# Issuing each group of TensorE products in one piece in a decode attention and bilinear MLP kernel

## The chip, the cores and the metric

The kernel runs on one core of one Trainium2 chip. Times are device microseconds (us) of that core. Profiles are single executions, and each is marked fast or slow. On one core a run is called slow when it is over 1.5% above the fastest run of the same kernel. The granted clock of TensorE in the records is 1.0 or 0.5, and its mean over an execution is given beside the span.

## The reference, cut to what matters

Two tokens (B=2, one query each) go through attention over a cached context and through a bilinear MLP, forward and backward. All tensors are bf16.

```python
# D = 576, Hq = 32, Hkv = 16, Sk = 4096, Dh = 128, F = 4608
xn = layernorm(x)
q  = (xn @ wq).reshape(B, 1, Hq, Dh)
p  = softmax(q @ k_cache^T * Dh**-0.5)      # two query heads share a cache head
y  = x + (p @ v_cache) @ wo + ((xn @ w_gate) * (xn @ w_up)) @ w_down
# returned: y and, by jax.vjp with grad_out, the gradients of
# x, k_cache, v_cache, wq, wo, w_gate, w_up, w_down
```

In all 92.48 MB are read and 92.48 MB written. The two caches and their two gradients are almost three quarters of that, 67.1 MB each way; the weights and their gradients are nearly all the rest. Per step (4 cache heads of one batch entry, 16 steps) TensorE does four things that matter here:

- **scores**: a full-array product (128 rows, 128 columns) of a cache tile that VectorE has transposed, in halves of 16 products, 2048 in all;
- **contractions**: the weighted sum over the cache (128 rows, 32 columns), 64 products each, 32 of them;
- **outer products**: the gradient of the cache (32 rows, 128 columns), in units of 8, each copied out of PSUM by ScalarE or VectorE and then written;
- pieces of the **weights'** work, of several shapes.

Rows and columns are those of the array that a product uses. Where they differ from one product to the next, I call it a change of shape. From the last product before it to the first one after it, start to start, the traces show a longer gap than between products of one shape: 147 to 149 ns at full clock and 241 ns at half (medians, kernel before). I call that gap a drain. That is a name for the time alone: what TensorE does in it isn't shown.

## The kernel before

The code is Python that builds an instruction list. A scheduler puts each engine's instructions in order, so the loops below don't say what lies next to what on TensorE. In particular, the scores of a slot, the outer units queued with `more(2)` and the contraction all feed one queue.

```python
def head_scores(n, t, x, s_ps, half):
    X = xtile([P, NCH, 64], "X")                       # 3 buffers
    t32(...)                                           # VectorE transposes half a cache tile
    for e in range(2):
        be = 2 * half + e
        for c8 in range(8):                            # 16 products, 128 rows x 128 columns
            nc.tensor.matmul(s_ps[:], lhsT=view(W[t][:], ...), rhs=view(X[:], ...), start=..., stop=...)

def contract(rowsT, heads):
    o_ps = ps_m([P, Dh])                               # "m": 2 buffers in PSUM
    for c4 in range(4):
        for c8 in range(8):
            for x, head in enumerate(heads):           # 64 products, 128 rows x 32 columns
                cg = 2 * x + c8 % 2
                nc.tensor.matmul(o_ps[32 * cg:32 * cg + 32, :], lhsT=view(rowsT[:], ...),
                                 rhs=head[:, 8 * c4 + c8, :], start=..., stop=...)
    ...                                                # copied out; the cache tiles come free

def unit(x, ch, A):                                    # one outer unit
    def f():
        ...
        o = ps_o()                                     # 2 buffers of 128 x 1024
        for c in range(4):
            for aa in range(2):                        # 8 products, 32 rows x 128 columns
                a = 2 * A + aa
                nc.tensor.matmul(o[:, aa, c * Dh:(c + 1) * Dh], lhsT=rows[32 * a:32 * a + 32, 4 * ch + c, :],
                                 rhs=bd[32 * a:32 * a + 32, x * Dh:(x + 1) * Dh], start=True, stop=True)
        evac(st[...], o[:], 1024)                      # ScalarE or VectorE
        if ch == 1 and A == 1:
            nc.gpsimd.dma_start(oview[b, :, :, l0 + x]..., st[:]...)
    return f

def slot(src, t, b, l, s_ps, per, mid=None):
    n = head_load(src, b, l)                           # 1 MB of cache, 12 buffers
    head_scores(n, t, l % 2, s_ps, 0)
    more(2)                                            # two outer units
    if mid:
        mid()                                          # softmax or contraction of earlier heads
    head_scores(n, t, l % 2, s_ps, 1)
    more(2)
    other(per)                                         # a piece of the weights' work
    return n
```

(Arguments are cut where "..." stands.)

## Time and profile before

| | before |
|---|---|
| runs at first | 550.19, 550.38, 558.83 us |
| profiled execution | 561.93 us (span 560.2), slow, mean clock 0.766 |
| TensorE products / changes of shape in its order | 8921 / 684 |
| pieces that the 32 contractions are issued in | 76 |
| pieces that the 128 score halves are issued in | 254 |

The three counts are taken from the built instruction list in TensorE's order. Strictly, 684 counts the stretches of one shape; the changes between them are one fewer, 683. The same holds for every such count from a built list below. The lines of the profile are in the prediction below.

### The profile page before, as it was taken

The page shows a single profiled execution, that of the slowest core. Times are in us where ns is not written, and L with a number is a line of the kernel's source. Part 1 is how long each engine was busy: PE and PEld are TensorE (multiplying, and loading weights), DVE is VectorE, ACT ScalarE, POOL GpSimd, SP SyncE. Part 2 cuts the span into 40 slices and gives each one's busy share as a digit, 9 for nine tenths or more (in the row PEclk, how much of TensorE's full clock was granted, in tenths as well). Part 3 has the DMA queues.
Part 4 walks back from the last instruction along what each step waited for, and adds up shares of the span by engine and source line. Part 5 has one row for each costly group of instructions (what it writes and reads, how often), then busy time and mean ns, then how long its engine had stood idle before and what let it go on. Part 6 is the DMA issues. An engine that isn't in the chain of part 4 may idle for free.

```text
span 560.2 us, 20059 instructions
## 1 busy us (share of the span) xinstructions
PE 475.7 (85%) x8921; PEld 362.5 (65%) x8921; DVE 362.0 (65%) x624; ACT 330.6 (59%) x454; POOL 204.6 (37%) x372
## 2 busy tenths in 40 slices
PE   0588988998989999888989899998888999879873
PEld 0476766776776677666767667776776757767630
DVE  8685655757657646458575675668676646577564
ACT  1135695857566465567565665667555566566553
POOL 5125252432622521624235243344243243351322
PEclk9988798877787555688787975589888566798955
DMA  8993999999699998699997999979979889764546
GB/s 254 411 385 135 355 412 368 397 381 405 227 403 393 384 366 324 213 388 379 353 391 253 417 415 375 393 279 411 392 294 390 356 291 403 283 239 171 219 152 245
DMA packets 52911, 186.26 MB, mean 333 GB/s; under 512 B 4140, under 2 KB 19128, under 8 KB 44632
## 3 DMA queue, kind: packets, MB, share of 16 engines
q1 hardware_dynamic: 28392, 92.49, 44.3%
q0 software_dynamic: 24432, 92.48, 43.0%
q8 instruction: 70, 1.15, 0.8%
q14 instruction: 17, 0.14, 0.1%
HBM read 92.48 MB, written 92.48 MB: 330 GB/s over the span
## 4 chain that ended last, share of the span: by engine, by line
PE 31%; ACT 9%; issue 5%; DVE 4%; POOL 2%; POOLq 0%; DVEq 0%; ACTq 0%
PE ps_sc L503 11%; ACT so L93 8%; PE ps_o L549 6%; PE ps_m L518 4%; PE ps_m L527 1%; POOL prm L533 1%; PE ps_m L440 1%; PE ps_o L681 1%; DVE so L90 1%; PE ps_o L651 1%; DVE sto L90 1%; PE ps_m L272 1%; PE ps_o L364 1%; PE ps_m L618 1%; DVE X L102 1%
## 5 line engine op out<-in xcount | busy, mean ns | idle before, releaser
L93 ACT CAST so<-ps_o 128x1024 bf16<-128x1024 f32 x232 | 225.1, 1019 | 125.5 <-PE ps_o L549 114.0
L503 PE MATMUL ps_sc<-X,W 128*128 128x128 bf16 x2048 | 197.2, 249 | 5.3 <-DVE X L102 4.5
L102 DVE STREAM_TRANSPOSE X<-kv 128x1024 f32<-128x1024 f32 x128 | 157.6, 1233 | 44.1 <-PE ps_sc L503 42.7
L503 PEld LDWEIGHTS <-W 128*128 128x128 bf16 x2048 | 153.1, 112 | 27.7 <-issue 17.5
L553 POOL DMA_DIRECT2D out_dram<-so x64 | 50.0, 781 | 138.5 <-ACT so L93 74.6
L549 PE MATMUL ps_o<-bd,dsm 32*128 32x128 bf16 x1024 | 50.9, 245 | 10.3 <-ACT so L93 5.8
L518 PE MATMUL ps_m<-kv,rowT 128*32 128x128 bf16 x2048 | 59.3, 272 | 0.0
L549 PE MATMUL ps_o<-bd,prm 32*128 32x128 bf16 x1024 | 46.3, 250 | 14.3 <-POOL prm L533 7.0
L518 PEld LDWEIGHTS <-rowT 128*32 128x32 bf16 x2048 | 43.0, 121 | 10.0 <-issue 5.8
L549 PEld LDWEIGHTS <-dsm 32*128 32x128 bf16 x1024 | 30.4, 104 | 24.8 <-issue 18.4
L549 PEld LDWEIGHTS <-prm 32*128 32x128 bf16 x1024 | 27.8, 105 | 26.8 <-issue 13.5
L533 POOL TENSOR_TENSOR prm<-pr,maskc 128x1024 bf16<-128x1024 bf16 x16 | 30.2, 1888 | 36.5 <-DVE pr L580 36.5
L93 ACT CAST stw<-ps_o 128x1024 bf16<-128x1024 f32 x28 | 27.8, 1028 | 13.8 <-PE ps_o L364 12.6
L474 POOL COPY dM<-qd 128x128 bf16<-128x128 bf16 x32 | 9.3, 289 | 73.1 <-PE ps_m L480 46.2
L90 DVE CAST so<-ps_o 128x1024 bf16<-128x1024 f32 x24 | 29.1, 1211 | 8.7 <-PE ps_o L549 8.2
L467 POOL COPY W<-rep 32x16 bf16<-32x16 bf16 x128 | 24.7, 193 | 26.1 <-PE ps_sc L503 18.9
L533 POOL TENSOR_TENSOR dsm<-ds,maskc 128x1024 bf16<-128x1024 bf16 x16 | 30.2, 1889 | 4.6 <-DVE ds L600 4.0
L93 ACT CAST std<-ps_o 128x576 bf16<-128x576 f32 x36 | 22.8, 646 | 12.6 <-PE ps_o L397 12.4
L102 DVE STREAM_TRANSPOSE Xw<-wgu 128x1152 f32<-128x1152 f32 x18 | 24.5, 1360 | 4.1 <-PE ps_sc L503 4.0
L93 ACT CAST sto<-ps_o 128x576 bf16<-128x576 f32 x25 | 15.6, 642 | 14.1 <-PE ps_o L681 13.9
L719 DVE TENSOR_SCALAR oT<-ps_m 128x4 bf16<-128x4 f32 x16 | 2.7, 171 | 29.6 <-PE ps_m L527 29.6
L371 POOL DMA_DIRECT2D out_dram<-stw x18 | 13.5, 752 | 19.0 <-ACT stw L93 10.6
(178 smaller groups left out, 591.8 us busy)
## 6 DMA issues: line engine op xcount, KB each, us to landing
out_dram<-so POOLq DMA_DIRECT2D x64, 1024.0 KB, 9.5
kv<-in_A_k_cache_dram SPq DMA_DIRECT2D x32, 1024.0 KB, 11.8
kv<-in_A_v_cache_dram SPq DMA_DIRECT2D x32, 1024.0 KB, 10.1
out_dram<-stw POOLq DMA_DIRECT2D x18, 512.0 KB, 9.3
wd<-in_B_w_down_dram SPq DMA_DIRECT2D x9, 576.0 KB, 12.7
out_dram<-std POOLq DMA_DIRECT2D x9, 576.0 KB, 7.9
wo<-in_A_wo_dram SPq DMA_DIRECT2D x4, 1152.0 KB, 13.4
wgu<-in_B_w_gate_dram SPq DMA_DIRECT2D x9, 512.0 KB, 14.0
```

What stands on the lines that cost most here:

```text
L90: nc.vector.tensor_copy(out=out, in_=in_)
L93: nc.scalar.copy(out, in_)
L102: nc.vector.transpose(out, in_)
L272: nc.tensor.matmul(dp[32 * gq:32 * gq + 32, 0:P], lhsT=view(Wm[:], 0, P, 8 * pos(q, s), [[1, 32]]), rhs=view(X[:], 0, P, koff(s) * 256 + ( ...
L371: nc.gpsimd.dma_start(out[0:512, f0:f0 + FS].rearrange("(c p) n -> p c n", p=P), st[:])
L467: nc.gpsimd.tensor_copy(view(W[t][:], 32 * a, 32, 28 + 32 * a, [[2 * WW, 4], [WW + 2, 2], [1, 2]]), view(st["rep"][:], 32 * a, 32, t * 4 * ...
L474: nc.gpsimd.tensor_copy(view(dM[:], 0, P, t * 2 * P, [[P + 2, 2], [4, 32], [1, 2]]), view(st["qd"][:], 0, P, (2 if t == 0 else 1) * GH * 2 ...
L503: nc.tensor.matmul(s_ps[:], lhsT=view(W[t][:], 0, P, (be * 2 + x) * WW + 28 - 4 * c8, [[1, P]]), rhs=view(X[:], 0, P, c8 * 64 + e, [[8 * 6 ...
L518: nc.tensor.matmul(o_ps[32 * cg:32 * cg + 32, :], lhsT=view(rowsT[:], 0, P, c4 * 32 + 4 * c8, [[1, 32]]), rhs=head[:, 8 * c4 + c8, :], sta ...
L533: nc.gpsimd.tensor_tensor(m[:], view(rows[:], 0, P, 0, [[0, 8], [1, P]]), view(maskc[:], 0, P, 0, [[1, 8], [0, P]]), ALU.mult)
L549: nc.tensor.matmul(o[:, aa, c * Dh:(c + 1) * Dh], lhsT=rows[32 * a:32 * a + 32, 4 * ch + c, :], rhs=bd[32 * a:32 * a + 32, x * Dh:(x + 1) ...
L553: nc.gpsimd.dma_start(oview[b, :, :, l0 + x].rearrange("a m n -> m a n"), st[:].rearrange("p a c d -> p a (c d)"))
```

## The change

Every group of products is wrapped in a `Block`. Its first product is issued as before. The others are issued after it and at top priority, so the scheduler has no reason to put another ready product between them. The aim is fewer changes of shape. The core of the diff:

```diff
+    class Block:
+        def __init__(self):
+            self.first, self.stack = None, ExitStack()
+        def __enter__(self):
+            return self
+        def __call__(self, *args, **kwargs):
+            ins = nc.tensor.matmul(*args, **kwargs)
+            if self.first is None:
+                self.first = ins
+                self.stack.enter_context(tc.issue_after(ins.ins))
+                self.stack.enter_context(tc.high_priority())
+        def __exit__(self, *exc):
+            self.stack.close()
 ...
-        for e in range(2):
-            be = 2 * half + e
-            for c8 in range(8):
-                nc.tensor.matmul(s_ps[:], ...)
+        with Block() as mm:
+            for e in range(2):
+                be = 2 * half + e
+                for c8 in range(8):
+                    mm(s_ps[:], ...)
 ...      (the same for contractions, outer units and every group of the weights' work)
```

All these products now have the line of the helper in the profile, so they are told apart by their tiles: `ps_sc<-X,W` is a score, `ps_m<-kv,rowT` a contraction, `ps_o<-bd,prm` or `ps_o<-bd,dsm` an outer product.

## The prediction

> **What bounds the kernel now.** The times come first: 550.19, 550.38 and 558.83 us. The profiled run took 561.93 us (span 560.2) and is marked slow, so the 550.38 that I predict against belongs to a quicker execution than the one I read, by about 11 us. Then the page, for the balance of the engines:
>
> ```profile
> PE 475.7 (85%) x8921; PEld 362.5 (65%) x8921; DVE 362.0 (65%) x624; ACT 330.6 (59%) x454; POOL 204.6 (37%) x372
> PEclk9988798877787555688787975589888566798955
> q1 hardware_dynamic: 28392, 92.49, 44.3%
> q0 software_dynamic: 24432, 92.48, 43.0%
> ```
>
> Two resources are near full: TensorE (85% busy, with the granted clock falling to 0.5 for long stretches) and the 16 DMA engines. The packets of all queues take 44.3 + 43.0 + 0.8 + 0.1 = 88.2% of the span, 494 us. In the trace a packet of 8192 bytes takes 309 ns in almost every stretch, so these 494 us are occupancy and not queueing. The span can hardly fall below 494 us plus the start and the tail, whatever TensorE does.
>
> Third, the waits, to see which of the two leads, first those of all engines and then those of the load queue:
>
> ```profile
> ACT so L93 <- PE ps_o L549: 114.0, 94, 4.9
> DVE X L102 <- PE ps_sc L503: 42.7, 36, 4.7
> PEld L549 <- issue: 32.0, 99, 0.8
> PEld L503 <- issue: 17.5, 72, 0.7
> PE ps_o L549 <- ACT so L93: 11.7, 27, 0.8
> PE ps_o L549 <- POOL prm L533: 7.0, 6, 1.4
> ...
> SPq L491 <- PE ps_m L518: 208.9, 19, 20.4
> ```
>
> ScalarE and VectorE wait for TensorE; TensorE waits for others little (11.7 and 7.0 us are its largest waits after the start); and the loads of the cache wait 208.9 us for buffers that the contraction (L518) frees. No compute engine waits for a load worth naming. So TensorE leads, and the DMA engines follow at a distance of a few per cent. The busy table by stretch (columns: stretch; busy time and count of PE, PEld, DVE, ACT, POOL; granted clock; DMA share; GB/s) gives that distance:
>
> ```profile
> 20.00:480.00 460.00, 412.94 (x7695) 317.72 (x7699) 295.08 (x492) 285.22 (x395) 171.37 (x315) 0.76 0.93 354
> 192.00:233.00 41.00, 38.17 (x649) 28.36 (x649) 21.52 (x39) 24.21 (x32) 16.03 (x26) 0.58 0.86 318
> 500.00:560.00 60.00, 42.59 (x813) 28.11 (x813) 36.63 (x65) 32.03 (x41) 18.43 (x25) 0.69 0.54 199
> ```
>
> The DMA share is 0.93 over the long middle, 0.86 where the clock is 0.58, and 0.54 in the tail, which only writes. Fourth, the timeline of the weight loads in a slow-clock stretch:
>
> ```profile
> 200.63 0.34 PEld L364 LDWEIGHTS <-xnr 32*128 32x128 bf16 x8 [0.20 <-issue]
> 201.17 0.56 PEld L503 LDWEIGHTS <-W 128*128 128x128 bf16 x6 [0.20 <-issue]
> 201.92 0.34 PEld L364 LDWEIGHTS <-xnr 32*128 32x128 bf16 x8 [0.20 <-issue]
> 202.46 0.56 PEld L503 LDWEIGHTS <-W 128*128 128x128 bf16 x6 [0.20 <-issue]
> ```
>
> Each time the products change from the full array (128*128) to 32 rows (32*128) and back, the weight loads pause 0.20 us and wait for nothing that the profile shows. A score half of 16 products is cut here into pieces of 6, and every cut pays twice.
>
> [...] From the last product of one shape to the first of the next, start to start, the median is 147 ns at full clock and 241 ns at half, against 58 and 104 ns between neighbouring full-array products, 26 and 43 between outer products, 14 and 25 in a contraction. [...] the clock records are 1.0 or 0.5 in multiples of 3.413 us, 76 or so windows at half and 80 at full. I sorted the windows by what followed. Half-clock windows followed by full clock (24) held 2.75 shape changes and 20 full-array products on average; those followed by half again (52) held 4.85 changes and 11. So cut-up stretches seem to hold the clock down; that is a correlation, not yet a cause. [...] the wait of ScalarE for TensorE (114.0 us) against 11.7 us the other way shows that evacuation is not what binds today.
>
> **The change part by part.** No product, copy or transfer is added or removed. Within a block, each product after the first must be issued after it and at top priority, so nothing slips between. I compared the two issue orders, classing each product by the rows and columns it uses. Runs of one kind of product go from 887 to 658; runs of ps_sc products become whole halves of 16 (before: 254 runs for 128 halves), and the contractions whole pieces of 64 (before: 76 runs for 32). Changes of shape go from 684 to 490: 194 fewer. The order of loads on their queue is unchanged.
>
> Drains saved: 365 of the old changes fell at full clock and 318 at half. Excess over ordinary spacing: 147 - (58+26)/2 = 105 ns at full, 241 - (104+43)/2 = 167 ns at half; weighted 0.53 x 105 + 0.47 x 167 = 134 ns. 194 x 0.134 = 26 us of TensorE's queue.
>
> Clock: with 28% fewer changes I expect the mean clock of a comparable run to go from 0.77 to about 0.81. Of 460 us in the middle, 5% is 23 us of TensorE time. As only a correlation carries it, I count 10 us. Together 36 us of relief on TensorE.
>
> What of it reaches the end: in the middle the DMA share can rise from 0.93 to about 1.02 (the table shows 1.02 for 14 to 28 us), which caps the gain at 460 x (1 - 0.93/1.02) = 41 us in the profiled run, and at some 30 us in a quick one, which has already used 11 of them. Of 36 us under a cap of 30, with the queues never perfectly fed, I take half: 15 us. The tail: its changes also fall (about 2 us), but in the new order outer products lag the contractions, by 1 to 13 units at each contraction, and 2.75 more of them stand behind the last one. At 1.02 us of ScalarE copy each that is 3 us. Net -15 - 2 + 3 = -14 us: about 536 us.
>
> **The rivals.** First, DMA takes over at once. The 494 us of packets speak for it; against it stands that no engine waits for a load today. It would leave 5 to 8 us of gain: 543 to 546 us, loads landing late as the new wait. Second, evacuation takes over. The new order issues outer units mostly in pairs (146 bursts of two against 108, and single units 45 against 136); a pair needs both ps_o buffers, and its copies take 2 x 1.02 = 2.04 us, while 16 scores, 16 outer products and two changes take 16 x 0.058 + 16 x 0.026 + 2 x 0.147 = 1.64 us at full clock. TensorE would then wait 0.4 us a pair, 146 x 0.4 = 58 us at the very worst, most of what was gained; but at half clock the same pair takes 16 x 0.104 + 16 x 0.043 + 0.48 = 2.83 us, so copies bind only where the clock is up, and contractions lie between. That gives 540 to 555 us. Third, the small products of the softmax chain (maximum, bias, sum) now wait for the end of a block: 4 per step, 16 steps, half a block of about 0.9 us each, 29 us of latency. Most of it is hidden behind the outer products queued meanwhile; waits of the mask (POOL prm, 36.5 us on DVE pr) would grow. Fourth, on the good side, the clock stays up nearly everywhere and the middle runs at the DMA limit: 517 to 522 us.
>
> **Range and chances.** Point 536 us. The low end, 517, is the whole 30 us of the middle and a little of the tail; the high end, 553, is the second rival with an unlucky clock. Faster by over 2% means under 539.4 us, only 3 us above my point, so 0.57; within 2%, where the first two rivals lie, 0.38; slower than 561.4 would need waits larger than all that is saved: 0.05.
>
> **What would show it.** Right: about 490 changes of shape; "issue" idle before the weight loads of outer and score products clearly under 32.0 and 17.5 us; a mean clock above 0.77 and no stretch of 40 us at 0.6; DMA share of the middle at 0.97 or more; a tail no shorter than now. Wrong: if the clock stays at 0.77 with fewer changes, the correlation was not a cause; if TensorE's wait for ScalarE's copies grows from 11.7 us to 40 or more, pairs took back the gain; if transposes start to wait for cache loads, DMA took over earlier than I allow; and if "issue" idle doesn't fall, the order on the chip is not the one I counted.

## The result, and the profile after

The changed kernel ran in 521.49, 524.13, 525.22 and 526.14 us: median **524.67 us**. The ratio to the kernel before is **0.949**, with a 95% interval of 0.940 to 0.958. A ratio here is the mean time of one kernel's fast runs over that of the other's fast runs of the same rounds, so it is not quite the ratio of the medians. The point predicted was 536 us and the range 517 to 553.

The profile of before is a slow execution. For a comparison I use the profile of a variant, the first experiment below, which has the block helper without the priority. Its TensorE order is the order of before, product for product, its time is the same (ratio 1.004) and its profiled execution is fast. I call it the old order. Here are the page of the old order and that of the changed kernel, each with the busy lines, the clock in 40 slices and the two large DMA queues (packets, MB, share of the 16 engines' span):

```profile
span 549.5 us, 20059 instructions
...
PE 460.2 (84%) x8921; PEld 351.7 (64%) x8921; DVE 360.7 (66%) x624; ACT 329.8 (60%) x454; POOL 204.7 (37%) x372
...
PEclk9998697978796655758798787599789997899555
...
q1 hardware_dynamic: 28392, 92.49, 45.5%
q0 software_dynamic: 24432, 92.48, 43.3%
```

```profile
span 519.7 us, 20063 instructions
...
PE 420.8 (81%) x8921; PEld 336.3 (65%) x8921; DVE 359.8 (69%) x624; ACT 327.5 (63%) x454; POOL 205.4 (40%) x372
...
PEclk9989999679959778796588995889898988799755
...
q1 hardware_dynamic: 28392, 92.49, 47.5%
q0 software_dynamic: 24432, 92.48, 45.0%
```

The other engines do the same work in the same time; TensorE is busy 39 us less. The deep dip of the clock in the middle of the old order (slices of 5 and 6) is gone. The busy table by stretch shows it, for the old order and then for the changed kernel (columns as in the prediction: stretch; PE, PEld, DVE, ACT, POOL; clock; DMA share; GB/s):

```profile
192.00:233.00 41.00, 38.18 (x635) 28.12 (x633) 21.65 (x39) 24.44 (x33) 14.97 (x24) 0.58 0.88 321
20.00:450.00 430.00, 382.42 (x7475) 295.88 (x7477) 281.99 (x474) 271.57 (x378) 164.85 (x301) 0.81 0.95 359
```

```profile
192.00:233.00 41.00, 35.32 (x790) 28.64 (x789) 28.64 (x50) 29.60 (x39) 16.91 (x30) 0.87 0.97 376
20.00:450.00 430.00, 365.96 (x7846) 298.48 (x7847) 294.44 (x499) 280.56 (x394) 173.53 (x316) 0.85 0.98 379
```

From 192 to 233 us the old order does 635 products at clock 0.58; before, in its slow execution, did 649 at the same 0.58, so this dip belongs to the order. The changed kernel does 790 there at 0.87, with less busy time. Over any 40 us of the middle the clock records of the old order fall to 0.50 at the lowest (from 183 us on), those of the changed kernel to 0.67. The DMA share of the middle rises from 0.95 to 0.98.

The waits (engine, line, what it waited for: us in total, times, longest), the old order first:

```profile
ACT so L114 <- PE ps_o L96: 111.8, 92, 5.0
PEld L96 <- issue: 87.2, 263, 2.3
...
POOL prm L566 <- DVE pr L614: 33.9, 16, 7.3
...
PE ps_o L96 <- ACT so L114: 17.1, 41, 1.1
```

```profile
PEld L93 <- issue: 91.7, 196, 3.8
...
ACT so L112 <- PE ps_o L93: 60.0, 71, 3.4
...
PE ps_o L93 <- ACT so L112: 20.5, 45, 1.2
...
POOL prm L564 <- DVE pr L612: 15.1, 12, 5.9
...
DVE Xd L121 <- DMA wd<-in_B_w_down_dram: 9.9, 2, 6.6
...
DVE X L121 <- DMA kv<-in_A_k_cache_dram: 5.4, 3, 2.8
```

ScalarE now waits for TensorE 60.0 us where it waited 111.8, and TensorE for ScalarE hardly more than before, 20.5 against 17.1. The mask on GpSimd waits less for the softmax, not more. VectorE now waits for loads before it transposes: 9.9 us for the weight tile `wd`, 2.2 in the old order, and 5.4 us for cache tiles, none there. The pauses called "issue" are fewer (196 against 263), but their sum didn't fall.

The timeline of weight loads in a stretch of the changed kernel at half clock (start, us, engine, line, operation, tile, count, idle time before) shows blocks kept whole:

```profile
208.46 1.75 PEld L93 LDWEIGHTS <-W 128*128 128x128 bf16 x16
210.40 0.37 PEld L93 LDWEIGHTS <-dsm 32*128 32x128 bf16 x16 [0.20 <-issue]
```

Where before had pieces of 6 scores and 8 outer products with a pause at each joint, there are 16 and 16 with one pause.

**TensorE's queue, added up.** I cut the time from the first product's start to the last one's into the gaps from start to start. A gap between products of one shape counts as stream, a gap at a change of shape as drain, one after an fp32 product apart; whatever a gap has over 65 ns (stream) or 155 ns (drain) at full clock, 110 or 250 at half, counts as stall. These caps are my choice, set just above the medians of the traces. In us:

```
                 first-last   stream (at full, at half)   drain (changes: full, half)   fp32   stall
before (slow)       541.8     294.7  (146.6, 148.2)       129.7  (376, 307)             20.1    97.3
old order           531.2     282.6  (166.1, 116.5)       123.1  (450, 233)             19.7   105.8
changed             501.3     283.7  (189.1,  94.6)        86.2  (371, 118)             20.4   111.0
```

From the old order to the changed kernel: drains -37, stream +1, stalls +5, in all -30 us. The medians of a gap at a change of shape stay what they were, 147 to 149 ns at full and 241 ns at half clock. The drains fell by more than the 28% of the changes because fewer of the remaining ones fall at half clock: 118 of 489, against 233 of 683.

### The profile page after: what moved, and what is told of

The parts are those of the page before. It is cut to its first block, busy times and chain, and to the rows that moved or that the text cites.

```text
span 519.7 us, 20063 instructions
## 1 busy us (share of the span) xinstructions
PE 420.8 (81%) x8921; PEld 336.3 (65%) x8921; DVE 359.8 (69%) x624; ACT 327.5 (63%) x454; POOL 205.4 (40%) x372
## 3 DMA queue, kind: packets, MB, share of 16 engines
q0 software_dynamic: 24432, 92.48, 45.0%
HBM read 92.48 MB, written 92.48 MB: 356 GB/s over the span
## 4 chain that ended last, share of the span: by engine, by line
PE 46%; DVE 16%; ACT 15%; DMA 9%; issue 9%; SPq 3%; POOL 1%; POOLq 0%; DVEq 0%; ACTq 0%
PE ps_sc L93 17%; ACT so L112 13%; PE ps_o L93 12%; PE ps_m L93 11%; DVE X L121 5%; DMA wd<-in_B_w_down_dram 4%; DMA out_dram<-so 3%; DVE so L109 2%; SPq L317 2%; PE ps_m L558 2%; DVE x_f L168 1%; DMA wgu<-in_B_w_gate_dram 1%; DVE Xd L121 1%; ACT stw L112 1%; PE ps_m L509 1%
## 5 line engine op out<-in xcount | busy, mean ns | idle before, releaser
L93 PE MATMUL ps_sc<-X,W 128*128 128x128 bf16 x2048 | 159.0, 236 | 13.4 <-issue 6.7
L93 PEld LDWEIGHTS <-W 128*128 128x128 bf16 x2048 | 141.4, 106 | 21.1 <-issue 14.5
L93 PE MATMUL ps_m<-kv,rowT 128*32 128x128 bf16 x2048 | 44.0, 250 | 3.8 <-issue 3.2
L93 PEld LDWEIGHTS <-rowT 128*32 128x32 bf16 x2048 | 36.8, 112 | 6.5 <-issue 4.3
L564 POOL TENSOR_TENSOR prm<-pr,maskc 128x1024 bf16<-128x1024 bf16 x16 | 30.3, 1891 | 15.2 <-DVE pr L612 15.1
L93 PEld LDWEIGHTS <-Wdy 128*128 128x128 bf16 x306 | 22.3, 111 | 4.6 <-POOL dM L503 3.1
L396 POOL DMA_DIRECT2D out_dram<-stw x18 | 13.7, 759 | 29.0 <-ACT stw L112 13.9
L555 ACT COPY o_sb<-ps_m 128x128 f32<-128x128 f32 x32 | 8.6, 269 | 25.1 <-PE ps_m L93 24.8
## 6 DMA issues: line engine op xcount, KB each, us to landing
out_dram<-so POOLq DMA_DIRECT2D x64, 1024.0 KB, 10.6
```

The lines of the kernel that those rows point to most:

```text
L93: ins = nc.tensor.matmul(*args, **kwargs)
L396: nc.gpsimd.dma_start(out[0:512, f0:f0 + FS].rearrange("(c p) n -> p c n", p=P), st[:])
L555: nc.scalar.copy(o_sb[:], o_ps[:])
L564: nc.gpsimd.tensor_tensor(m[:], view(rows[:], 0, P, 0, [[0, 8], [1, P]]), view(maskc[:], 0, P, 0, [[1, 8], [0, P]]), ALU.mult)
```

## The experiments

Twelve kernels ran, in three groups on the same chip each with runs of before beside them. The expectations name theories by letter. In short: theory A puts the gain down to the number of changes of shape alone; C to how the outer units lie between the contractions; D to the cuts inside contractions. B was a rival of A in the first group, and both expected a gain from scores alone. Groups differ by chip: e1 to e8 ran on one chip, e9 to e12 on another. A table of what came out; the changes and the pieces are counted in the built instruction list:

| label | blocks whole | changes | contraction pieces | median us | ratio to before [95%] | profiled span, clock |
|---|---|---|---|---|---|---|
| before | none | 684 | 76 | 551 to 555 | 1 | 560.2, 0.766 (slow) |
| after | all | 490 | 32 | 524.67 | 0.949 [0.940, 0.958] | 519.7, 0.840 |
| e1 | none, edge only | 684 | 76 | 555.27 | 1.004 [0.994, 1.015] | 549.5, 0.809 |
| e2 | scores | 615 | 109 | 558.46 | 1.006 [0.996, 1.016] | 555.3, 0.806 |
| e3 | contractions | 652 | 32 | 534.29 | 0.962 [0.953, 0.972] | 533.6, 0.824 |
| e4 | all but outer | 495 | 32 | 520.92 | 0.941 [0.933, 0.950] | 520.6, 0.853 |
| e9 | all but contractions | 593 | 111 | 552.76 | 0.997 [0.988, 1.005] | 550.9, 0.787 |
| e10 | scores and contractions | 548 | 32 | 534.76 | 0.967 [0.959, 0.975] | 531.3, 0.819 |

**e1: the ordering edge without the priority.**

```diff
                 self.stack.enter_context(tc.issue_after(ins.ins))
-                self.stack.enter_context(tc.high_priority())
```

> The blocks keep their ordering edge (each product after the first must follow the first) but lose the top priority. By the instruction order it is the kernel before, product for product: 684 changes of array shape. If the contiguity does the work: the same time as before, ratio 0.99 to 1.01, and its profile serves as one of the old order in whatever clock state the chip is in (mean clock near 0.77). If the edge itself helped, by dropping waits: 0.95 to 0.98.

Measured: 1.004, the same as before. The built lists tell why: with the edge alone TensorE's order is that of before in every place. A variant with the priority and without the edge, which I only built, has the order of the changed kernel in every place. So the priority does all of the change and the edge nothing. As e1 is the old order with a new line number, its profile serves as the fast-state profile of before.

**e2, e3 and e4: one kind of block at a time.** The helper gets a kind and acts only for the kinds named.

```diff
+    BLOCKS = "s"          # e2 scores;  e3 "c" contractions;  e4 "scw" all but outer units
 ...
-            if self.first is None:
+            if self.on and self.first is None:      # self.on = kind in BLOCKS
```

> Only the score halves are issued in one piece: 615 changes of shape, 69 of the 194 that the whole change removes. Theory A (the drains at a change of shape are what counts, each alike): 69/194 of 28 us, about 10 us, ratio near 0.98. Theory B (keeping score products together is what matters[...]): most of the gain, ratio 0.95 to 0.965. Theory C (the gain is the new interleaving, in which outer products lag the contractions, 190 units done at a contraction's end on average against 196): nothing, as the lag here is 195.5: ratio 0.995 to 1.005.

> Only the contractions are issued in one piece: 652 changes of shape, 32 fewer. Theory A: 32/194 of 28 us, about 5 us, ratio near 0.99. Theory B (score products together): nothing. Theory C (outer products lag, contractions free the cache buffers earlier): 194.2 units done at a contraction's end, a third of the lag, so a third of the gain, ratio 0.98 to 0.985.

> All blocks except those of the outer products: 495 changes of shape, against 490 with all, and the same lag (189.7 units). Theories A and C both: the whole gain within 3 us, ratio 0.945 to 0.96. If it were the pairing of outer products that helps ScalarE's copies: much less, ratio 0.97 or more.

Measured: 1.006, 0.962 and 0.941. The first is a clear miss of A and B; only C had it. Scores alone take 69 changes away and gain nothing; contractions alone take 32 away and gain 3.8%, where no theory had more than 2%. Leaving the outer units alone costs nothing.

The profile of e2 shows the miss. Outer products still slip into contractions, more of them than before: 598 outer products lie inside contractions in the trace of e2, 334 in that of the old order. No score does in either. Here are the weight loads of one contraction of e2:

```profile
118.83 0.14 PEld L96 LDWEIGHTS <-rowT 128*32 128x32 bf16 x7 [0.20 <-issue]
119.16 0.10 PEld L96 LDWEIGHTS <-xnr 32*128 32x128 bf16 x1 [0.20 <-issue]
119.44 0.34 PEld L96 LDWEIGHTS <-xnr 32*128 32x128 bf16 x7 [0.18 <-issue]
119.98 0.24 PEld L96 LDWEIGHTS <-rowT 128*32 128x32 bf16 x12 [0.20 <-issue]
120.42 0.34 PEld L96 LDWEIGHTS <-prm 32*128 32x128 bf16 x8 [0.20 <-issue]
120.96 0.24 PEld L96 LDWEIGHTS <-rowT 128*32 128x32 bf16 x12 [0.20 <-issue]
```

and one of the changed kernel, also from the middle of the run:

```profile
110.28 1.17 PEld L93 LDWEIGHTS <-rowT 128*32 128x32 bf16 x64 [0.20 <-issue]
```

In e2 the 64 products of this contraction come in pieces of 7 to 13, with outer products between, and it ends only after 124 us. The mean time from the first to the last product of a contraction is 2.3 us in the old order, 2.9 in e2, 1.1 in e3 and 1.2 in the changed kernel. The waits of e2 show who waits longer:

```profile
DVE X L124 <- PE ps_sc L96: 65.0, 40, 6.1
...
POOL W L499 <- PE ps_sc L96: 48.2, 17, 7.9
```

VectorE waits 65.0 us to transpose the next cache tile, against 41.0 in the old order, and GpSimd 48.2 against 17.1, both for scores that TensorE hasn't done. VectorE's wait for `wd` is about as long here (9.4 us) as in the changed kernel, though e2 gains nothing and its DMA share of the middle is only 0.92 (0.95 in the old order).

**e9 and e10: the contraction taken out, and the two large kinds together.** They were made to tell "the contraction must be whole" from "the number of changes".

```diff
-    BLOCKS = "s"
+    BLOCKS = "sow"        # e9 all but contractions;  e10 "sc" scores and contractions
```

> All blocks except those of the contractions: 593 changes of shape (91 fewer than before), score halves whole, but the contractions cut into 111 pieces, more than the 76 of before; lag as before (195.5 units). Theory A (drains, each alike): 91/194 of 28 us, ratio near 0.975. Theory D, made after e2 and e3 (what counts is the whole contraction; blocks elsewhere push the cuts into it): no gain, ratio 0.99 to 1.01, stalls of TensorE up as in e2.

> Blocks for score halves and contractions only: 548 changes of shape (136 fewer), 32 contraction pieces. Theory A: 136/194 of 28 us, ratio 0.965. Theory D: at least what e3 gave, and once the contraction is whole the scores' saved drains should show too, which they did not alone: ratio 0.945 to 0.955.

Measured: e9 0.997, e10 0.967. With 593 changes, 91 fewer than before, e9 gains nothing: theory A, by the count alone, has fallen twice. D had the time of e9 right but not its sign, more stalls (105.3 us against 105.8, below), and it missed e10, which has 104 changes fewer than contractions alone and is no faster (0.967 against 0.962). C, the place of the outer units, fits the ranking of the first four variants but not the size of e10: 190.6 units are done at the end of a contraction on average there, 189.7 in the changed kernel (0.949) and 194.2 in e3 (0.962).

The queue account of these variants says where saved drains went:

```
             first-last   stream (at full, at half)   drain (changes: full, half)   fp32   stall
old order       531.2     282.6  (166.1, 116.5)       123.1  (450, 233)             19.7   105.8
e2              537.0     292.6  (168.0, 124.6)       111.6  (412, 202)             16.1   116.7
e9              532.4     300.0  (159.0, 141.0)       110.7  (376, 216)             16.5   105.3
e3              515.3     279.9  (174.8, 105.1)       114.4  (455, 196)             19.6   101.5
e10             512.9     287.7  (176.3, 111.4)        98.9  (369, 178)             18.7   107.6
e4              502.2     277.6  (196.3,  81.3)        85.5  (390, 104)             19.0   120.0
changed         501.3     283.7  (189.1,  94.6)        86.2  (371, 118)             20.4   111.0
```

e2 and e9 save 12 us of drains each; in e9 17 us come back as streaming (25 more at half clock, 7 less at full), in e2 10 as streaming and 11 as stalls. e3 loses 9 of drains, 4 of stalls and 3 of streaming: no single term makes its 16 us.

**e5 and e6: changes of shape added at a fixed order.** To price a change by itself, each score half of the changed kernel gets one tiny product in its middle: in e5 of 32 rows, which makes two changes of shape, in e6 of 128 rows, which makes none. The 256 tiny products are the same otherwise (2 columns of output, into an unused corner of the PSUM tile).

```diff
-        return ps.tile([P, P], FP32, tag="sc", ...)
+        return ps.tile([P, P + 4], FP32, tag="sc", ...)
 ...                                       # after product c8 == 3 of each eight:
+                    if c8 == 3:
+                        mm(s_ps[:, P:P + 2], lhsT=ident[0:32, :], rhs=ident[0:32, 0:2], start=False, stop=False)
                                           # e6: ident[0:128, :] and ident[0:128, 0:2]
```

> The changed kernel with one tiny product (2 columns, into unused columns of the score bank) after the 4th product of every 8 of a score half: 256 products on 32 rows, so that each costs two changes of shape, 512 more in all (about 1000). The result stays right. Its twin e6 has the same order with the tiny product on all 128 rows and no added change. Theory A (drains): 512 x 0.105 to 0.167 us is 54 to 86 us of TensorE's queue more than the twin; less the slack that the DMA-bound middle leaves (some 20 us), it is 35 to 65 us slower than the twin, and the clock falls below 0.80. Theory C (interleaving only): as fast as the twin.

> The twin: the same 256 tiny products, on all 128 rows, no added change of shape. 256 x about 0.06 us is 15 us of TensorE at most; under theory A most of it hides in the slack: 0 to 8 us slower than the changed kernel, ratio to the kernel before 0.95 to 0.965, clock 0.82 to 0.85.

Measured: medians 566.77 and 527.73, 39 us apart. Of e5's four runs three are over the limit for fast and its profile is one of those; its one fast run, 555.71, is 29 us above the mean of the three fast runs of e6, 526.31. Both ways the 512 added changes cost far more than the tiny products themselves (e6 is within 2 or 3 us of the changed kernel). Since only one run of e5 was fast, its size is uncertain; C, which expected no difference, misses.

**e11 and e12: the same in contractions.** Theory D asked for a higher price there. The tiny products go into each contraction, after products 2 and 5 of each eight: 512 changes in e11, none in e12.

```diff
-        o_ps = ps_m([P, Dh])
+        o_ps = ps_m([P, Dh + 4])
 ...
+                    if c8 in (2, 5):
+                        mm(o_ps[0:P, Dh:Dh + 2], lhsT=ident[0:32, 0:P], rhs=ident[0:32, 0:2], start=False, stop=False)
                       # e12: o_ps[0:32, Dh:Dh + 2], lhsT=ident[0:P, 0:32], rhs=ident[0:P, 0:2]
```

> The changed kernel with 8 tiny products in each contraction, 256 in all, on 32 rows: 512 added changes of shape, about 1000 in all, as in e5 but inside the contractions. Theory A: like e5, 35 to 45 us slower than its twin e12. Theory D: a cut there delays a chain that others wait for, so 50 us or more slower than the twin.

> The twin of e11: the same order, the 256 tiny products on all 128 rows and 32 columns, as the contraction's own, no added change. Within 1.5% of the changed kernel under either theory: ratio to the kernel before 0.94 to 0.965.

Measured: medians 579.63 and 540.47, again 39 us apart; the fast runs 578.77 (three) and 535.25 (two), 44 apart. e12 itself came out slower than I had expected, 11 us above the changed kernel by fast runs: eight more products in each contraction cost more than the tiny products of e6 did in scores, and I can't say why.

The pages' busy lines of the four kernels, in the order e5, e6, e11, e12, show what the added changes do to TensorE:

```profile
PE 490.1 (87%) x9177; PEld 368.9 (65%) x9177; DVE 359.7 (64%) x624; ACT 328.9 (58%) x454; POOL 205.3 (36%) x372
```

```profile
PE 426.6 (82%) x9177; PEld 343.9 (66%) x9177; DVE 354.4 (68%) x624; ACT 328.3 (63%) x454; POOL 206.4 (40%) x372
```

```profile
PE 500.2 (87%) x9177; PEld 376.9 (65%) x9177; DVE 359.1 (62%) x624; ACT 328.8 (57%) x454; POOL 204.8 (36%) x372
```

```profile
PE 438.3 (82%) x9177; PEld 353.1 (66%) x9177; DVE 359.5 (67%) x624; ACT 328.2 (61%) x454; POOL 204.6 (38%) x372
```

The same 9177 products occupy TensorE 64 and 62 us longer; the other engines work as before. In the queue account the drains grow by 76 us in each pair and the stalls shrink by 25: the engine spends in drains what it would have spent waiting. So a change of shape costs: 29 to 44 us for 512, or 0.06 to 0.085 us each end to end, of the 0.15 that it takes in the queue. D asked for 50 us or more in contractions, and that did not come. Whether the price is the same in both places isn't shown: the medians agree at 39, the fast runs (29 and 44) do not, and the 29 hangs on one run.

This prices the count, around the changed kernel; that the price holds at the old order too is assumed. By it 194 changes fewer are worth 11 to 16 us, about half of the gain measured. For e3 it says 2 to 3 us, where 21 were measured (3.8%); for e2 4 to 6, where none came; for e10 6 to 9 more than for e3, where none came either. The count is one cause, shown at a fixed order, and it isn't the whole.

**e7 and e8: the DMA engines relieved.** Before and changed kernel, each writing only half of every cache gradient tile. Their outputs are wrong, which doesn't matter for the times. Two of four slices are left out.

```diff
-                    nc.gpsimd.dma_start(oview[b, :, :, l0 + x].rearrange("a m n -> m a n"),
-                                        st[:].rearrange("p a c d -> p a (c d)"))
+                    nc.gpsimd.dma_start(oview[b, 0:2, :, l0 + x].rearrange("a m n -> m a n"),
+                                        st[:, 0:2].rearrange("p a c d -> p a (c d)"))
```

> The kernel before, with only half of each cache-gradient tile written out (32 MB less of 186; wrong result on purpose), all compute unchanged: 693 changes of shape. If TensorE led before, as predicted: little faster, ratio 0.97 to 1.00. If the DMA engines led: 0.85 to 0.92 (their packets would take about 410 us instead of 494).

> The changed kernel with the same half of the writes: 494 changes of shape. If the middle of the changed kernel is at the DMA limit (its share is 0.98 there against 0.93 before), this gains more than e7 did: ratio to the kernel before 0.90 to 0.93, 5 to 20 us below the changed kernel, and e8 to e7 shows the whole relief on TensorE, 36 to 50 us. If TensorE still leads: within 1% of the changed kernel.

Measured: before with half the writes 555.77 us (ratio 1.012, interval 1.004 to 1.020), so no gain; the changed kernel with half the writes 499.66 us (0.908), 25 below the changed kernel with all, where 5 to 20 were expected. The busy table of the middle, e7 and then e8:

```profile
20.00:480.00 460.00, 411.46 (x7962) 320.80 (x7963) 299.20 (x503) 291.10 (x404) 174.75 (x323) 0.79 0.82 302
```

```profile
20.00:480.00 460.00, 403.21 (x8800) 325.53 (x8800) 329.86 (x564) 319.89 (x444) 190.59 (x343) 0.85 0.83 313
```

With 18% fewer bytes to move (152.8 instead of 186.3 MB; HBM written falls from 92.48 to 58.92 MB) the kernel before keeps its time and lets the DMA engines idle: share 0.82. They did not bound it. The changed kernel at the same low share goes 25 us faster than with all writes: a part of its time is the DMA engines'. Two caveats. Fewer bytes also land sooner, and so free the staging buffers sooner: the median write of `so`, half as large, landed 5.9 us after its issue in e7, against 9.5 in before, and 8.1 in e8, against 10.6 in the changed kernel. So the relief isn't of bandwidth alone. And e7 isn't quite the order of before: it has 693 changes for 684 and 86 contraction pieces for 76, and its fast runs have a mean clock of 0.770 where those of before in the same rounds have 0.791. In the queue account its stalls are 10 us fewer than in the old order, and streaming and drains 9 us more. So the relief reached TensorE and was lost again there; with the order and the clock held, e7 might have gained some of it.

**Is there a better version?** e4 leaves the outer units out of the change and is the fastest that ran: 520.92 us, 0.941 [0.933, 0.950]. Its interval overlaps that of the changed kernel, so it is not shown to beat it. It is the smaller change at the same time.

## Why the prediction was right or wrong

**The bound was right.** TensorE led and the DMA engines followed at a few per cent. That the DMA engines did not lead is shown by e7, that they follow close by e8 against the changed kernel; e5 and e11 show that more changes on TensorE cost the changed kernel time.

**The relief of TensorE's queue was right.** The prediction had 26 us of drains over ordinary spacing, and 10 of clock. The account shows drains -37; the 194 gaps that stopped being changes are now ordinary ones, and at the prediction's own 42 to 74 ns each they put some 10 us into the stream, so net about 27. The stream grew by only 1 instead of 10, so by this estimate the clock gave back about 9. (The line between the two is loose: some 4 or 5 us of the 27 are the clock's too, as fewer of the remaining changes fall at half clock.) The prediction's guess of the mean clock, "from 0.77 to about 0.81", was right in its step and low in both ends: 0.784 over the four runs of the old order, 0.832 over those of the changed kernel. One detail of its sum is loose: the 147 and 241 ns are medians, but the spacings taken off them (58 and 26, 104 and 43) are nearer to means; the medians in the same trace are 57 and 19, 107 and 7. That moves the 26 us to about 28.

**What reaches the end was mis-sized.** The step is "Of 36 us under a cap of 30, with the queues never perfectly fed, I take half: 15 us". The last product of the last contraction started at 516.3 us in the old order and at 483.7 in the changed kernel: 32.6 us arrived, not 15, and a little over the cap of 30. The tail after it grew from 33.2 to 36.0 us, by 2.8, where the prediction had 3 less 2, so 1. Together 29.8 us of span, where the prediction had 14. Two of its assumptions did not hold. First, it took the packets' 494 us as fixed. By the shares of the pages shown above they took 89.7% of 549.5, or 493 us, in the old order (q1, q0 and 0.9% of the two small queues), and 93.4% of 519.7, or 485 us, in the changed kernel: 8 us of occupancy went away with the same bytes. Why, I don't know. Second, the half stood for queues "never perfectly fed"; TensorE's stalls rose by 5 us and no more, and the DMA share of the middle went to 0.98, close to the 1.02 of the cap. The half itself was a guess, and with it the point came out 11 us above the measured time.

**The DMA limit is real all the same.** With half the writes the same change is worth 56 us (554.9 to 498.7 by fast runs, ratio 0.899). Against before itself the changed kernel with half the writes is 51 us faster by fast runs (549.3 to 498.7), which leaves e7's own order out. With all writes the change is worth 28 us, by the ratio and by the medians (553.31 over all four runs of before; the prediction started from 550.38, the median of the first three). About half of what TensorE could gain does reach the end, then, but half of 51 to 56. With all writes the queue account has only 36 us of relief (drains -37, stream +1), as the prediction had it; with half of them it has 48 (e7 to e8: drains -41, stream -7, stalls 0; 693 and 494 changes as built). The changed kernel and e8 differ by 19.5 us from the first product to the last; 16 of them are stalls, 3 streaming, and drains are alike. So in these two executions the DMA limit shows as stalls of TensorE, not as a lower clock (0.840 and 0.844); over the fast runs the clock is 0.832 and 0.858. The 15 us was too small either way.

**The rivals.** DMA takes over at once: partly so, as e8 shows, but only after most of the gain had come. Its sign, transposes that wait for cache loads, came too (5.4 us in three waits), and there are three gaps of over 3 us between products in the middle (old order: none), two of them behind a load that VectorE waited for. These are weak signs: e2, with no gain and a DMA share of 0.92, has the same wait for `wd`, 2.6 us for cache tiles, and three such gaps. The third gap, 3.8 us at 422.5 us in the middle of a score half, waits for nothing that the profile shows. Evacuation takes over: no; TensorE's wait for ScalarE's copies is 20.5 us against 17.1, not 40 or more. The softmax chain is delayed: the mask's wait fell from 33.9 to 15.1 us. The clock stays up nearly everywhere: half so, 0.85 in the middle with no stretch of 40 us under 0.67.

**Signs that were named.** About 490 changes, a higher clock, a DMA share of 0.97 or more and a tail no shorter all came. One sign failed: the idle time called "issue" ahead of weight loads was to fall clearly, and it is 91.7 us against 87.2, in fewer and longer pauses. Taken by tile, it rose from 28.7 to 42.6 us ahead of the outer products of the cache and from 13.9 to 14.5 ahead of scores. By the prediction's own rule that should mean another order on the chip than the one counted; the changes in the trace, 489, are as many as in the built list, so the order is the one. The sum of such pauses is then not a measure of changes; what else it holds isn't shown.

**What the prediction didn't see** is that the count it built on doesn't rank the variants. 615 and 593 changes gain nothing, 652 gain 3.8%, 548 no more than 652. In every variant that gains, the contractions are whole. That is what the runs show; why it is so, they don't settle. One argument is that a cut contraction lets go of cache tiles late and holds up everything that waits for them (contractions of 2.9 to 3.0 us in e2 and e9, 1.1 to 1.2 where whole). Against it, e11 cuts contractions further, to 3.2 us, and by medians its pair costs no more than the pair in scores; by fast runs it costs 14 us more, with one run of e5. Nor is it settled why the weights' groups bring 0.967 to 0.941 from e10 to e4. Each variant is also another order from the scheduler, in more than the one thing named.

Whether the clock is a cause or a companion stays open too. In each pair of equal order, e5 and e6, e11 and e12, the kernel with more changes has the lower clock in its profile (0.785 and 0.833, 0.787 and 0.803; e5's is a slow execution), so more changes went with a lower clock both times, but no run held the clock and varied the rest. The traces do show what the clock goes with. It is not long pauses: in the kernel before 64 of the 133 windows of 3.413 us (the step of the clock records) from 20 to 480 us are at half clock, though no two neighbouring products there start more than 2.34 us apart; and from 192 to 233 us, where the clock is 0.58, TensorE is busy 38.17 of 41 us and no two start more than 1.02 us apart. Nor is it the number of full-array products: of the 718 windows with 26 or more of them, over all 14 profiles, 133 were followed by one at half clock. But count for each product the share of the array that it uses (rows times columns, each rounded up to 32, 64 or 128, over 128 times 128) times its columns of `rhs` over 128, and add this up in each window of the 14 profiles. The 517 windows with less than 20 such units were all followed by one at half clock, the 1007 with 26 or more all by one at full clock; the 583 between by either. Every order of the same products does 3889 units in all, and a window in the middle (20 to 480 us) holds 26.2 on average in the old order, 28.1 in the changed kernel. That is a correlation. Whether in a kernel so close to 26 a small loss of time also costs clock, so that one saved pause is worth more in one order than in another, no run tested.

## What to carry to other kernels

Compare orders, not just counts: a scheduler that saves a switch in one group may push more cuts into another, as the scores-only variant did to the contractions. Price a disputed cost by adding it twice, once with and once without the property in question, at an otherwise fixed order; here that gave 0.06 to 0.085 us for a change that takes 0.15 in the queue. When two resources are within a few per cent of each other, relieve the second in both kernels: it shows which one leads, as far as the order stays the same, and how much of the first one's gain the second one takes. Put the granted clock and the number of changes of shape beside the busy shares: the busy share of weight loads hardly saw this change, 64% in the old order and 65% in the changed kernel, while the clock went from 0.809 to 0.840, the changes from 684 to 490 and the time down by 5%. The order of the queue mattered by itself here: the orders that were run, with the same 8921 products and all writes, have medians between 520.92 and 558.46 us.
